# Sums of w_val's low parts in the transposes' banks, a first load in two parts, P.V apart from the scores in two early groups, and new urgencies for the list order

## The chip, the cores and the metric

One core of a Trainium2 chip runs the whole program. The metric is the time of one execution on the device in microseconds (us), the median of several runs. TensorE (PE in the rows) multiplies, VectorE (DVE) and ScalarE (ACT) work elementwise, GpSimd (POOL) helps them out of SBUF, and SyncE (SP) issues the loads and stores.

## The reference, cut to what matters

```python
scores = 1.0 / np.sqrt(D) * np.matmul(q, k.transpose(0, 1, 3, 2))      # B, H, S, D = 4, 8, 768, 64
keep = (pos[None, :] < 8) | ((rel >= 0) & (rel < 96))                  # 8 global keys and 96 local ones
scores = np.where(keep, scores + bias, -1e9)                           # bias: -slope of the head * distance
a = softmax(scores)
x = np.matmul(a, v).transpose(0, 2, 1, 3).reshape(B, S, H * D)
gate = sigmoid(sum(conv_w[k] * xp[:, k:k + S] for k in range(5)))      # causal taps along the sequence
out = (gate * (x @ w_val)) @ w_out                                     # w_val, w_out: 512 x 512
```

## The kernel before, in words

The work falls into 32 groups: four batches, two halves of the sequence of 384 rows (`hf`), four pairs of heads. Four groups with the same batch and half make a phase (`ph`, 8 of them). A group has three steps of 128 query rows, 96 steps in all.

For a group, `load` brings keys and queries (tile `kq`), and `scores` (the row of products that is called S below) fills two PSUM banks `s`. For each step and each head of the pair, VectorE adds the bias and takes the row minimum (`add_bias`, tiles `t` and `mins`), ScalarE takes the exponential and its sum (`expo`, tiles `p` and `sm`), GpSimd or VectorE adds 1e-9 to the sum (`guard`), VectorE inverts it (`recip`, `rs`), and GpSimd or VectorE scales the probabilities (`norm`, written to `p`). TensorE transposes them into one of two banks `pt` (`transpose`), ScalarE or VectorE copies that out (`evac_pt`, tile `a`), and `pv` multiplies with the values, two groups at a time, into the banks `x` (called P.V below). From `x` come the high part `xh` (ScalarE), the low part `xl` (VectorE) and five taps of the convolution (`conv`, tile `gate`; ScalarE does the first, VectorE the rest). Per phase follow `val` (`x @ w_val`, 48 matmuls), the product with the gate (`gated`, tile `g`), its parts `gh` and `gl`, and `outp` (36 matmuls, tile `o`), in two banks that have the tag "moe".

Matrix products of full precision are made from three products of rounded parts, so each weight needs a high and a low part. The weights come as 64-bit floats. `f64_abs`, `f64_op` and `w_high` rebuild them in eight pieces (numbers 0 to 3 are w_val, 4 to 7 w_out), and `w_sum` forms the low part on TensorE as a sum of three products (tile `wsum`), which ScalarE or VectorE copies out. For w_val these sums sit in the "moe" banks, for w_out in the banks of the transposes.

What runs when is set by `Plan`: each operation has an urgency, the engines that may do it with a cost for each, and the operations it depends on. `Plan.order` walks through time: it takes the engine that can start something soonest and gives it the ready operation of least urgency. `SPARE` shifts the choice between engines that may do the same operation. The order that comes out is fixed when the program is built; on the chip each engine works down its own list, and waits where an input is late. From group 4 on, P.V of the pair before is tied to the scores of an odd group: it stands directly ahead of them on TensorE, and it also waits for what they wait for (`ALONE`, `follow`).

`zeros` and `transpose` also issue products of ones whose result is not used (8 at the start, 3 after the first scores, some ahead of early transposes).

Of the kernel before, what the change touches and what calls it, by code (L numbers as in the profile page):

```python
# [15 lines left out]
AX = mybir.AxisListType  # L16
WARM = 8
S_B, PT_B, X_B = 2, 2, 2
U_D1, RAW_B = -5.67, 4
FILL_UNTIL = 80.0  # L20
FILL_N, FILL_TO, U_F = 1, 1, -0.93
W_AT = (-0.83, 5.35, 7.09, 10.66, 17.84, 19.21, 23.25, 35.21)
W_PARTS = (2, 2, 2, 2, 2, 2, 1, 1)
# [3 lines left out]
U_XE, U_XH, U_CV, CV_STEP = -0.29, 0.48, 4.06, 0.71  # L27
U_AM, U_EX, U_RC, U_PT, U_EV, U_MOE = -0.83, 0.3, -4.29, -1.16, 4.27, 19.31
LAG, ALONE = 2, 4
U_L, U_LV, U_WL, U_S, U_HI, U_NM = -21.15, -0.46, -9.19, -2.28, 1.27, -0.88  # L30
U_PH = (-5.11, -0.44, -0.85, -0.71, -0.86, -0.58, -4.31, 2.92)
U_SG, U_GM, GM_STEP, U_GH, U_GL, U_O, VAL_T, O_T, U_OE = 14.07, -1.19, -0.47, 0.06, 0.36, 2.94, 5.39, 4.03, 1.99
PSUM = bass.MemoryType.PSUM
# [26 lines left out]
class Plan:  # L60
# [28 lines left out]
    def order(self, start):  # L89
# [16 lines left out]
        while avail:  # L106
            cands = []
            for i in avail:
# [4 lines left out]
            _, i, e = min(  # L113
                ((ops[i][0], i, e) for t, i, e in cands if e == first[2] and t <= first[0] + 1e-9)
            )
# [23 lines left out]
def attention_moe(ctx, tc, qT, kg, kq0, kq1, va0, va1, v, counts_in, wv, cw, wo, out):  # L139
# [84 lines left out]
    def load(g):  # L224

        b, hf, p = groups[g]
        n = kwidth(hf) + HT
        t = tile_of(("kq", g), [P, KQ], F32, "kq", RAW_B)
        nc.sync.dma_start(t[:, :n], (kq0, kq1)[hf][b, p])
        T["rk", g], T["rq", g] = t[:, : n - HT], t[:, n - HT : n]  # L230

    def load_v(g):
# [8 lines left out]
    for g, (b, hf, p) in enumerate(groups):  # L241
        key = ("L", g)
        plan.add(key, 3 * g + U_L, {SP: 0.5}, lambda e, g=g: load(g), plan.ring("kq", RAW_B, key, [("S", g)]),
                 P * (kwidth(hf) + HT) * 4)
# [127 lines left out]
    def w_sum(i):  # L372

        tag, bufs = ("moe", 2) if i < NC else ("pt", PT_B)
        high = wvh[:, i] if i < NC else woh[:, i - NC]
        ps = tile_of(("wsum", i), [P, DM], F32, tag, bufs, psum)
        nc.tensor.matmul(ps, ident, T[("w", i), "h"].bitcast(F32), start=True, stop=False)
        nc.tensor.matmul(ps, units[:, 1], high, start=False, stop=False)
        nc.tensor.matmul(ps, units[:, 0], T[("w", i), "r"], start=False, stop=True)

    def add_sum(i):
        key, low = ("WS", i), wvl[:, i] if i < NC else wol[:, i - NC]
        bank = plan.ring("moe", 2, key, [("WP", i)]) if i < NC else plan.ring("pt", PT_B, key, [("WP", i)])
        plan.add(key, W_AT[i] + 0.6, {PE: 1.6}, lambda e: w_sum(i), [("WH", i), ("W4", i), ("UNITS",)] + bank)
# [3 lines left out]
    for i in range(2 * NC):  # L388
# [14 lines left out]
        plan.add(("WH", i), u + 0.5, {ACT: 0.52, DVE: 0.335}, lambda e, i=i: w_high(e, i), [("W2", i), ("W3", i)])  # L403
        if i < NC:
            add_sum(i)

# [124 lines left out]
    def s_deps(g):  # L531
        deps = [("L", g)]
        return deps + ([("AM", 3 * (g - 1) + k, j) for k in range(HB) for j in range(2)] if g else [])
# [18 lines left out]
    for g in range(NGRP + LAG):  # L552
        gs = batches.get(g)
        if gs and ALONE <= g < NGRP:
            add_pv(gs, g, pv_cost(gs) + SWITCH, s_deps(g))
        elif gs:
            add_pv(gs, g, pv_cost(gs) + 2 * SWITCH)
        if g < NGRP:
            joined = gs and g >= ALONE
            plan.add(("S", g), 3 * g + U_S, {PE: s_cost(g) + 2 * SWITCH}, lambda e, g=g: scores(g),  # L560
                     s_deps(g) + ([("PV", gs[0])] if joined else []))
            if joined:
                plan.follow(("S", g), ("PV", gs[0]))

    for g, (b, hf, p) in enumerate(groups):
        for k in range(HB):
# [20 lines left out]
            for j in range(2):  # L587
# [5 lines left out]
                     [("NM", s, 0), ("NM", s, 1), ("IOTA",)] + bank, bank=bank)  # L593
            for i in range(NC, 2 * NC):
                if s == WS_AT[i - NC]:
                    add_sum(i)
# [352 lines left out]
def layouts(inputs):  # L949
# [28 lines left out]
    for hf, (lo, hi) in enumerate(((0, P + PER * (HB - 1)), (P + PER * (HB - 1) - TAIL, P + PER * (NB - 1)))):  # L978
        kq.append(np.concatenate([kT[..., lo:hi], qT[..., hf * HT : (hf + 1) * HT]], axis=-1))
        own = slice(0, HB - 1) if hf == 0 else slice(HB - 1, NB - 1)  # L980
        parts = [vs[:, :, :, own].reshape(B, NP, P, -1), vo[:, :, :, own].reshape(B, NP, P, -1)]
# [28 lines left out]
```

## Time and profile before

| what | value |
|---|---|
| median of 3 runs | 278.65 us (278.49 to 278.68) |
| the profiled execution, its own time | 278.04 us |
| its span, first to last instruction | 276.3 us |
| mean granted TensorE clock | 0.994 of full speed |
| TensorE busy with matmuls | 261.1 us (95%) |
| TensorE busy with weight loads | 215.9 us (78%) |
| ScalarE busy | 208.7 us (76%) |
| VectorE busy | 193.7 us (70%) |
| GpSimd busy | 129.9 us (47%) |

The profiled execution took 1.74 us more than its span, which lies ahead of the first and behind the last instruction. Busy times are shares of the whole span: an engine that is full in one stretch and half idle in the next shows a middling share, so the rows further down are taken by stretch. An idle time in a row is that of the engine just before the instruction, and the arrow names what ended it.

### The profile page before, as it was taken

The numbers are of one execution on the slowest core, as the hardware profiler recorded it, in microseconds if no ns is written. First come the engines' busy times: TensorE is split into PE (matmuls) and PEld (weight loads), VectorE is DVE, ScalarE is ACT, GpSimd is POOL, SyncE is SP. The second block draws the span as 40 slices with busy tenths as digits, with TensorE's granted clock in tenths as the row PEclk, the third lists the DMA queues.
The fourth block names the chain that finished last, engine by engine and source line by source line (L and its number), as shares of the span: only waits on it lengthen the run. The fifth ranks groups of instructions, "written<-read, shape, count | busy, mean of one in ns | idle before, by whom it ended". The sixth has DMA issues, their size and how long they took to land.

```text
span 276.3 us, 8766 instructions
## 1 busy us (share of the span) xinstructions
PE 261.1 (95%) x3113; PEld 215.9 (78%) x3114; DVE 193.7 (70%) x762; ACT 208.7 (76%) x700; POOL 129.9 (47%) x323
## 2 busy tenths in 40 slices
PE   7689899898899999999999999999999999999995
PEld 3366587766589788988899788888898888977984
DVE  3878999697938866595949684787849584844610
ACT  4999997897969688787878797887877786854321
POOL 5877526666344633374345633373346544350230
PEclk9899999999999999999999999999999999999999
DMA  6779884251735144421645164523551011001003
GB/s 171 275 240 303 290 302 149 92 151 59 241 121 183 62 149 143 148 94 55 223 116 191 40 193 138 157 66 119 178 187 65 4 76 40 2 2 77 38 2 122
DMA packets 16048, 36.36 MB, mean 132 GB/s; under 512 B 1920, under 2 KB 3968, under 8 KB 16000
## 3 DMA queue, kind: packets, MB, share of 16 engines
q1 hardware_dynamic: 16000, 35.75, 39.2%
q8 instruction: 27, 0.44, 0.7%
q14 instruction: 21, 0.17, 0.2%
HBM read 29.45 MB, written 6.29 MB: 129 GB/s over the span
## 4 chain that ended last, share of the span: by engine, by line
PE 57%; DVE 15%; ACT 2%; issue 1%; POOL 1%; POOLq 0%
PE o L693 23%; PE val L670 12%; PE x L512 7%; DVE gate L622 6%; PE pt L495 6%; PE s L451 5%; PE x L518 4%; DVE t L459 3%; DVE g L677 3%; DVE xl L614 2%; DVE p L484 1%; ACT gate L624 1%; POOL p L484 1%; ACT p L469 1%; ACT ob L704 0%
## 5 line engine op out<-in xcount | busy, mean ns | idle before, releaser
L484 POOL TENSOR_SCALAR p<-p,rs 128x168 f32<-128x168 f32 (+1 forms) x179 | 75.7, 435 | 43.2 <-DVE rs L479 35.4
L469 ACT ACTIVATE p<-t,mins 128x168 f32<-128x168 f32 (+1 forms) x192 | 82.0, 429 | 11.1 <-DVE mins L459 9.9
L622 DVE SCALAR_TENSOR_TENSOR gate<-x,cwt,gate 128x384 f32<-128x384 f32 x128 | 78.5, 614 | 1.0
L459 DVE CUSTOM_DVE_ANT_0 t<-s,bias 128x168 f32<-128x168 f32 (+1 forms) x192 | 56.7, 317 | 9.6 <-PE s L451 9.6
L495 PE MATMUL pt<-ident,p 128*128 128x128 f32 x272 | 49.1, 282 | 4.2 <-POOL p L484 3.3
L476 POOL TENSOR_SCALAR sm<-sm 128x2 f32<-128x2 f32 x92 | 19.5, 212 | 63.2 <-ACT p L469 57.3
L670 PE MATMUL val<-xh,wvh 128*128 128x384 f32 x128 | 47.6, 372 | 1.2 <-DVE g L677 1.2
L161 ACT COPY a<-pt 128x384 f32<-128x384 f32 (+1 forms) x96 | 43.6, 454 | 4.8 <-PE pt L495 4.8
L495 PEld LDWEIGHTS pt<-ident,p 128*128 128x128 f32 x272 | 34.1, 142 | 16.5 <-POOL p L484 9.2
L693 PE MATMUL o<-woh,gh 128*128 128x512 f32 (+1 forms) x100 | 42.5, 425 | 1.1 <-DVE g L677 0.9
L670 PE MATMUL val<-xh,wvl 128*128 128x384 f32 x128 | 43.1, 337 | 0.0
L670 PE MATMUL val<-xl,wvh 128*128 128x384 f32 x128 | 43.1, 337 | 0.0
L684 POOL TENSOR_TENSOR gl<-g,gh 128x384 fp32r<-128x384 f32 x29 | 29.2, 1010 | 26.8 <-ACT gh L161 25.7
L693 PE MATMUL o<-wol,gh 128*128 128x512 f32 (+1 forms) x100 | 38.9, 389 | 1.2 <-ACT wol L161 1.2
L693 PE MATMUL o<-woh,gl 128*128 128x512 f32 (+1 forms) x100 | 38.6, 386 | 0.0
L469 ACT ACTIVATION_READ_ACCUMULATOR p<-t,mins 128x1 f32 x192 | 37.1, 193 | 0.0
L451 PE MATMUL s<-kq 64*64 64x104 f32 (+3 forms) x1088 | 34.2, 262 | 3.0 <-DMA kq<-in_kq 3.0
L451 PEld LDWEIGHTS s<-kq 64*64 64x64 f32 x1088 | 30.3, 133 | 7.6 <-issue 4.0
L614 DVE TENSOR_TENSOR xl<-x,xh 128x384 fp32r<-128x384 f32 x32 | 17.3, 555 | 25.8 <-ACT gate L624 16.1
L161 ACT CAST xh<-x 128x384 fp32r<-128x384 f32 x32 | 15.1, 484 | 20.8 <-PE x L518 20.8
L479 DVE RECIPROCAL rs<-sm 128x2 f32<-128x2 f32 x96 | 15.5, 161 | 21.7 <-POOL sm L476 21.0
L670 PEld LDWEIGHTS val<-xh,wvh 128*128 128x128 f32 x128 | 24.1, 188 | 3.9 <-DVE g L677 2.4
(155 smaller groups left out, 373.1 us busy)
## 6 DMA issues: line engine op xcount, KB each, us to landing
kq<-in_kq SPq DMA_DIRECT2D x16, 444.0 KB, 4.3
kq<-in_kq SPq DMA_DIRECT2D x16, 392.0 KB, 4.3
va<-in_va SPq DMA_DIRECT2D x16, 384.0 KB, 4.2
out<-ob SPq DMA_DIRECT2D x24, 256.0 KB, 2.2
va<-in_va SPq DMA_DIRECT2D x16, 320.0 KB, 4.3
w<-in_wv SPq DMA_DIRECT2D x8, 256.0 KB, 4.4
w<-in_wo SPq DMA_DIRECT2D x4, 256.0 KB, 3.8
w<-in_wo SPq DMA_DIRECT2D x2, 512.0 KB, 3.9
```

Source lines behind the costliest of these rows:

```text
L161: nc.scalar.copy(dst, src)
L451: nc.tensor.matmul(s[rows, u : u + w], T["rq", g][r, k * P + half * QH : k * P + (half + 1) * QH], T["rk", g][r, c : c + w], start=True, s ...
L459: nc.vector.tensor_tensor_reduce(out=t[:, :n], in0=T["s", s // HB, s % HB, j][:, :n], in1=bias[:, h, :P] if n == P else bias[:, h, P:], op ...
L469: nc.scalar.activation(T["p", s][:, j, :n], T["t", s, j][:, :n], AF.Exp, bias=mins[:, s, j : j + 1], scale=-1.0, accum_out=T["sm", s][:, j ...
L476: engine(e).tensor_scalar(out=sm, in0=sm, scalar1=1e-9, scalar2=1.0, op0=ALU.add, op1=ALU.mult)
L484: engine(e).tensor_scalar(out=pr, in0=pr, scalar1=rs, scalar2=1.0, op0=ALU.mult, op1=ALU.mult)
L495: nc.tensor.transpose(pt[:, i * P : (i + 1) * P], pr[:, c : c + P], ident)
L614: engine(e).tensor_sub(tile_of(("xl", g), [P, HT], F32R, "xl", XH_B), T["x", g][:, HIST:], T["xh", g])
L622: nc.vector.scalar_tensor_tensor(out=gt, in0=src, scalar=w, in1=gt, op0=ALU.mult, op1=ALU.add)
L670: nc.tensor.matmul(T["val", ph, m], (wvh, wvh, wvl)[r][:, m, c * P : (c + 1) * P], (T["xh", g], T["xl", g], T["xh", g])[r], start=(c == 0 ...
L684: engine(e).tensor_sub(tile_of(("gl", ph, m), [P, HT], F32R, "gl", 5), T["g", ph, m], T["gh", ph, m])
L693: nc.tensor.matmul(T[key][:, cols], (T["gh", ph, c], T["gl", ph, c], T["gh", ph, c])[r][:, rows], (woh, woh, wol)[r][:, c, cols], start=(c ...
```

## The change

Six things change; what is computed stays the same.

1. The sums of w_val's low parts use the banks of the transposes, as those of w_out did. They are placed by step (`WS_AT`).
2. The first load of keys and queries is issued in two parts: columns 0 to 127 of both, then the rest. For that the array of the first half is padded to two equal parts of 400 columns. The scores of step 0 need the first part alone.
3. P.V is tied to the scores of an odd group only from group 9 on (`JOIN`), where it was from group 5 on. In groups 5 and 7 it is now an operation of its own.
4. At the start there are 10 products of ones and not 8, and after the first scores 12 and not 3.
5. All urgencies have new values, and `SHIFT` adds to each kind of operation a value of its own for each of the 8 phases.
6. `SPARE` has new values.

```diff
-WARM = 8
+WARM = 10
-FILL_N, FILL_TO, U_F = 1, 1, -0.93
+FILL_N, FILL_TO, U_F = 4, 1, -1.44
-WS_AT = (15, 19, 22, 24)
-SPARE = {'vector': 0.8, 'gpsimd': 0.02, 'scalar': -0.96}
+WS_AT = (1, 4, 7, 10, 15, 19, 22, 24)
+SPARE = {'vector': 0.91, 'gpsimd': 0.02, 'scalar': -1.19}
-LAG, ALONE = 2, 4
+LAG = 2
+JOIN = (0, 0, 0, 0, 1, 1, 1, 1, 1, 1, 1, 1, 1, 1, 1, 1)
+SHIFT = {
+    'AM': (-3.57, 0.0, 0.0, 0.0, 0.45, 0.94, 0.07, 3.21),
...
+        if key[0] in SHIFT:
+            urgency += SHIFT[key[0]][key[1] // PER_PHASE[key[0]]]
...
-        nc.sync.dma_start(t[:, :n], (kq0, kq1)[hf][b, p])
+        if g == 0:
+            load_part(slice(0, P))
+        else:
+            nc.sync.dma_start(t[:, :n], (kq0, kq1)[hf][b, p, :, :n])
...
+        if g == 0:
+            plan.add(("LB", 0), U_L, {SP: 0.5}, lambda e: load_part(slice(P, kwidth(0))))
...
-        tag, bufs = ("moe", 2) if i < NC else ("pt", PT_B)
+        ps = tile_of(("wsum", i), [P, DM], F32, "pt", PT_B, psum)
...
-        if gs and ALONE <= g < NGRP:
-            add_pv(gs, g, pv_cost(gs) + SWITCH, s_deps(g))
-        elif gs:
-            add_pv(gs, g, pv_cost(gs) + 2 * SWITCH)
+        join = JOIN[g // 2] if gs and g < NGRP else 0
+        pv_in = [d for h in gs for d in pv_deps(h)] if join == 2 else []
+        if join != 2 and gs:
+            add_pv(gs, g, pv_cost(gs) + SWITCH * (2 - join), s_deps(g) if join else [])
```

The order that comes out of it differs most in the first 10 groups. On ScalarE the exponentials of group 5 (the `p` tiles with the numbers 798 before and 730 now) stand as follows. Before, from the copy of step 12's transposes on:

```order
L161 COPY a_679<-pt_666 128x384
L332 ACTIVATE ('w', 4)_y<-w_495 128x512
L663 ACTIVATE gate_542<-gate_542 128x384 x2
L161 COPY a_730<-pt_690 128x384
L161 CAST woh<-('w', 4)_h 128x512
L161 CAST xh_763<-x_653 128x384
L161 COPY hist<-x_653 128x4
L161 CAST xh_768<-x_697 128x384
L161 COPY hist<-x_697 128x4
L624 ACTIVATE gate_542<-x_653,cwt 128x384
L332 ACTIVATE ('w', 5)_y<-w_613 128x512
L469 ACTIVATE p_798,sm_799<-t_0_787,mins 128x168
```

Now, from the copy of step 10's transposes on:

```order
L188 COPY a_678<-pt_636 128x384
L370 ACTIVATE ('w', 4)_y<-w_516 128x512
L188 CAST wvl<-wsum_664 128x512
L699 ACTIVATE gate_582<-gate_582 128x384
L188 COPY a_728<-pt_713 128x384
L504 ACTIVATE p_730,sm_731<-t_0_720,mins 128x168
L188 COPY a_741<-pt_723 128x384
L504 ACTIVATE p_730,sm_731<-t_1_733,mins 128x168
```

The pieces of weights 4 and 5, the high parts `xh` of groups 2 and 3 and their convolution moved from ahead of group 5's exponentials to behind them. Ahead of the first of them ScalarE now has one `f64_abs`, two `xh`, two small copies to `hist`, one `w_high`, three copies of transposes, one first tap and one tanh less, and one bias more. At the first exponential of group 9 the two lists hold the same work but for that one bias.

On TensorE the second place is around the scores of group 7 (`s` with the numbers 1040 before and 974 now) and P.V of groups 4 and 5 (`x` 894 and 965 before, 962 and 1052 now). Before:

```order
L495 MATMUL pt_984<-ident,p_913 128x128 x3
L512 MATMUL x_894<-a_679,va_486 64x128 x2
L512 MATMUL x_965<-a_890,va_544 64x128 x2
...
L518 MATMUL x_965<-a_967,va_544 64x64 x2
L451 MATMUL s_0_1040<-kq_662 64x168
...
L495 MATMUL pt_1074<-ident,p_939 128x128 x3
```

Now:

```order
L486 MATMUL s_0_974<-kq_705 64x168
...
L530 MATMUL pt_1000<-ident,p_870 128x128 x3
L729 MATMUL o_0_1012<-woh,gh_0_904 128x512
...
L416 MATMUL wsum_1042<-('w', 5)_r,units 128x512
L547 MATMUL x_962<-a_741,va_444 64x128 x2
L547 MATMUL x_1052<-a_935,va_561 64x128 x2
```

The scores of group 7 stood behind the transposes of step 18 and that P.V, and now stand ahead of both. P.V of groups 2 and 3 moved in the same way from ahead of the scores of group 5 to behind them.

The third place is TensorE's list near the end, at the last P.V (`x` 4509 before, 4551 now), the product `val` of phase 7 and `rmt`, the transpose of the check of the row minima. Before:

```order
L518 MATMUL x_4509<-a_4571,va_3862 64x64 x4
L693 MATMUL o_2_4574<-woh,gh_2_4483 128x512
...
L773 MATMUL rmt<-ident,row_max 1x128
L693 MATMUL o_2_4574<-woh,gh_3_4517 128x512
...
L670 MATMUL val_0_4629<-xh_4370,wvh 128x384
```

Now:

```order
L809 MATMUL rmt<-ident,row_max 1x128
L706 MATMUL val_0_4607<-xh_4430,wvh 128x384
...
L553 MATMUL x_4551<-a_4602,va_3875 64x64 x4
L706 MATMUL val_0_4607<-xh_4436,wvh 128x384
...
L706 MATMUL val_0_4607<-xh_4646,wvh 128x384
```

Six matmuls of `outp` that stood behind the last P.V now stand ahead of it, so `val` follows it at once; between the last P.V and the first `val` that needs its result (`xh` 4646) there are 12 other matmuls of `val`. On VectorE the list holds 6 normalisations of probabilities where it held 13, and no `guard` where it held 4; the rest went to GpSimd.

## Rows read from the trace of the kernel before

**Rows 1.** Windows: start:end, length, busy us (count) by engine, clock, DMA

```profile
5.79:39.09 33.30, 28.73 (x393) 20.83 (x387) 28.98 (x124) 31.81 (x112) 22.17 (x54) 0.95 0.85 285
...
39.09:70.43 31.34, 28.68 (x372) 21.60 (x372) 26.14 (x96) 26.52 (x89) 18.20 (x39) 1.00 0.40 130
...
96.58:156.89 60.31, 59.57 (x767) 51.62 (x768) 44.01 (x180) 48.21 (x166) 28.29 (x73) 1.00 0.41 133
```

**Rows 2.** The same view of two short stretches

```profile
50.00:54.70 4.70, 3.97 (x112) 3.38 (x113) 2.22 (x8) 3.40 (x11) 2.96 (x8) 1.00 0.30 112
...
65.00:70.43 5.43, 4.90 (x110) 3.83 (x111) 3.01 (x11) 4.05 (x13) 3.19 (x7) 1.00 0.18 51
```

**Rows 3.** Timeline: start us, us, engine line op, count [idle before <-releaser]

```profile
0.78 3.57 PE L254 MATMUL warm<-const-bfloat16-1.0 128*128 128x512 bf16 x8 [0.78 <-PEq L1000]
...
5.56 1.02 PE L451 MATMUL s<-kq 64*64 64x128 f32 x32 [1.20 <-DMA kq<-in_kq]
...
6.48 0.23 DVE L308 TENSOR_SCALAR dist<-m,counts 128x8 f32<-128x8 f32 x1
...
6.51 0.82 PE L254 MATMUL warm<-const-bfloat16-1.0 128*128 128x512 bf16 x3
...
9.12 1.14 PE L451 MATMUL s<-kq 64*64 64x128 f32 x32 [1.78 <-DMA kq<-in_kq]
...
12.06 0.27 DVE L459 CUSTOM_DVE_ANT_0 t<-s,bias 128x128 f32<-128x128 f32 x1
```

**Rows 4.** Windows by 5 us: the slice with a low clock

```profile
10.00:15.00 5.00, 4.53 (x26) 2.63 (x18) 4.47 (x25) 4.44 (x17) 4.14 (x10) 0.66 0.69 226
```

**Rows 5.** ScalarE's timeline: one of each kind, and the exponential opening group 5

```profile
5.79 1.77 ACT L320 ACTIVATE bias<-dist 128x128 f32<-128x128 f32 x7 [3.24 <-DVE dist L302]
...
33.20 0.52 ACT L161 COPY a<-pt 128x384 f32<-128x384 f32 x1
...
33.55 0.73 ACT L332 ACTIVATE ('w', 4)_y<-w 128x512 f32<-128x512 f32 x1
...
34.14 0.97 ACT L663 ACTIVATE gate<-gate 128x384 f32<-128x384 f32 x2
...
35.66 0.62 ACT L161 CAST woh<-('w', 4)_h 128x512 fp32r<-128x512 f32 x1 [0.19 <-DVE ('w', 4)_h L343]
...
36.52 0.48 ACT L161 CAST xh<-x 128x384 fp32r<-128x384 f32 x1 [0.24 <-PE x L518]
...
37.69 0.58 ACT L624 ACTIVATE gate<-x,cwt 128x384 f32<-128x384 f32 x1 [0.18 <-DVE xl L614]
...
39.09 0.44 ACT L469 ACTIVATE p<-t,mins 128x168 f32<-128x168 f32 x1
```

**Rows 6.** Timeline of ScalarE: two of its waits

```profile
46.13 0.44 ACT L469 ACTIVATE p<-t,mins 128x168 f32<-128x168 f32 x1 [0.81 <-DVE mins L459]
...
53.91 0.48 ACT L161 CAST xh<-x 128x384 fp32r<-128x384 f32 x1 [0.89 <-PE x L518]
```

**Rows 7.** Chain of waits (start us, us, what), then PE's timeline

```profile
89.47 1.00 DVE p L484
...
92.42 0.50 PE L693 MATMUL o<-woh,gh 128*128 128x512 f32 x1 [0.23 <-DVE g L677]
```

**Rows 8.** Waits of PE up to 100 us: total, times, longest us

```profile
PE pt L495 <- ACT wol L161: 0.3, 1, 0.3
```

**Rows 9.** Timeline: one sum of a low part, and its copy

```profile
18.14 1.02 PE L377 MATMUL wsum<-('w', 1)_h,ident 128*128 128x512 f32 x2
...
19.67 0.59 ACT L161 CAST wvl<-wsum 128x512 fp32r<-128x512 f32 x1 [0.28 <-PE wsum L379]
```

**Rows 10.** Timeline and chain of waits near the end

```profile
253.26 0.92 PE L518 MATMUL x<-a,va 64*64 64x64 f32 x24
...
255.27 0.56 DVE L614 TENSOR_TENSOR xl<-x,xh 128x384 fp32r<-128x384 f32 x1 [3.34 <-ACT gate L624]
...
255.86 8.55 PE val L670 x48
```

More of the change, by code (lines that the diff above doesn't have):

```diff
@@ L113, in order @@
             _, i, e = min(
-                ((ops[i][0], i, e) for t, i, e in cands if e == first[2] and t <= first[0] + 1e-9)
+                ((ops[i][0], i, e) for t, i, e in cands if e == first[2] and t <= first[0] + LOOK[e])
             )
@@ L228, in load, with load_part @@
         t = tile_of(("kq", g), [P, KQ], F32, "kq", RAW_B)
-        nc.sync.dma_start(t[:, :n], (kq0, kq1)[hf][b, p])
+        if g == 0:
+            load_part(slice(0, P))
+        else:
+            nc.sync.dma_start(t[:, :n], (kq0, kq1)[hf][b, p, :, :n])
         T["rk", g], T["rq", g] = t[:, : n - HT], t[:, n - HT : n]
+    def load_part(cols):
+        n = kwidth(0)
+        dst, src = (x[:, : 2 * n].rearrange("p (two n) -> p two n", two=2) for x in (T["kq", 0], kq0[0, 0]))
+        nc.sync.dma_start(dst[:, :, cols], src[:, :, cols])
     def load_v(g):
@@ L531, in s_deps @@
     def s_deps(g):
-        deps = [("L", g)]
+        deps = [("L", g)] + ([] if g else [("LB", 0)])
         return deps + ([("AM", 3 * (g - 1) + k, j) for k in range(HB) for j in range(2)] if g else [])
@@ L553, in attention_moe @@
         gs = batches.get(g)
-        if gs and ALONE <= g < NGRP:
-            add_pv(gs, g, pv_cost(gs) + SWITCH, s_deps(g))
-        elif gs:
-            add_pv(gs, g, pv_cost(gs) + 2 * SWITCH)
+        join = JOIN[g // 2] if gs and g < NGRP else 0
+        pv_in = [d for h in gs for d in pv_deps(h)] if join == 2 else []
+        if join != 2 and gs:
+            add_pv(gs, g, pv_cost(gs) + SWITCH * (2 - join), s_deps(g) if join else [])
         if g < NGRP:
-            joined = gs and g >= ALONE
             plan.add(("S", g), 3 * g + U_S, {PE: s_cost(g) + 2 * SWITCH}, lambda e, g=g: scores(g),
-                     s_deps(g) + ([("PV", gs[0])] if joined else []))
-            if joined:
-                plan.follow(("S", g), ("PV", gs[0]))
+                     s_deps(g) + ([("PV", gs[0])] if join == 1 else pv_in))
+        if join == 2:
+            add_pv(gs, g, pv_cost(gs) + SWITCH, [("S", g)])
+        if join:
+            plan.follow(*((("S", g), ("PV", gs[0])) if join == 1 else (("PV", gs[0]), ("S", g))))
     for g, (b, hf, p) in enumerate(groups):
@@ L593, in attention_moe @@
                      [("NM", s, 0), ("NM", s, 1), ("IOTA",)] + bank, bank=bank)
-            for i in range(NC, 2 * NC):
-                if s == WS_AT[i - NC]:
+            for i in range(2 * NC):
+                if s == WS_AT[i]:
                     add_sum(i)
@@ L979, in layouts @@
         kq.append(np.concatenate([kT[..., lo:hi], qT[..., hf * HT : (hf + 1) * HT]], axis=-1))
+        if hf == 0:
+            kq[0] = np.pad(kq[0], [(0, 0)] * 3 + [(0, hi - lo - HT)])
         own = slice(0, HB - 1) if hf == 0 else slice(HB - 1, NB - 1)
```

30 lines of the change are left out of this document (17 added, 13 removed), and 15 rows, old and new, of the table SHIFT.

## The prediction, made before the changed kernel ran

> **What bounds the kernel now.** I read the busy times by stretch first, cutting the span at the two points where the order before and after the change holds the same work. From 96.58 us on TensorE is the limit: in a period of two phases it is busy 59.57 of 60.31 us, with ScalarE at 48.21 and VectorE at 44.01 [rows 1]. Whatever the new urgencies do there can give at most the 0.74 us that TensorE idles per period. Its weight loads are busy 51.62 us of that period [rows 1], but the matmuls of `val` run 8.55/48 = 0.178 us apart with no gap [rows 10], and an order changes the gaps alone. The Trainium skill, Perfetto Trace Analysis, Identifying the Most-Contended Engine, holds that TensorE's matmul busy time is a poor measure of headroom and its weight loads' busy share a better one; by it the room would be 60.31 - 51.62 = 8.7 us a period. I weigh that as a rival below. Up to the first exponential of group 5, at 39.09 us [rows 5], it is another engine: ScalarE is busy 31.81 of 33.30 us, TensorE 28.73 [rows 1]. Between there and the first exponential of group 9, at 70.43 us, nothing is full: TensorE 28.68, ScalarE 26.52, VectorE 26.14 of 31.34 us [rows 1]. So a reader should look for a gain in the first 70 us, and ask of each edit whether it shortens ScalarE's list or its waits.
>
> Next I read those waits. ScalarE idles 33.30 - 31.81 = 1.49 us in the first stretch and 31.34 - 26.52 = 4.82 us in the second. Two holes hold 2.68 us of the latter: 50.00 to 54.70 (4.70 - 3.40 = 1.30) and 65.00 to 70.43 (5.43 - 4.05 = 1.38); VectorE idles 2.48 and 2.42 us in the same holes [rows 2]. Both are a joined P.V: TensorE waits for the last transposes before it, the scores stand behind it, and so VectorE has no scores and ScalarE no `x`, for which it waits 0.89 us at 53.91 [rows 6].
>
> **The change, part by part.** All sums are made against the profiled execution, 278.04 us, which is 0.61 us below the median of 278.65 us.
>
> First load in two parts: nothing. The scores of group 0 start at 5.56 us, when their load has landed [rows 3]; a smaller load may bring that forward. But the first `add_bias` stands behind the distances on VectorE, the last of which runs from 6.48 to 6.71 us [rows 3], and the new list keeps that order. If the distances were done sooner, the first scores would be worth up to their own wait, 1.20 us [rows 3]; the ends are 0 and -1.20, and I take 0, since the cover is in the list. The extra issue puts the next loads back a little; group 1's scores, which wait for theirs, have the slack of the next paragraph.
>
> Products of ones: nothing. Two more at the start take 2 x 3.57/8 = 0.89 us and end at 5.24, ahead of 5.56. Twelve after the first scores take 12 x 0.82/3 = 3.28 us at the pace of the three there now, so group 1's scores start at about 9.8 us, where they wait for a load until 9.12 [rows 3]. Their reader, the next `add_bias`, starts at 12.06 [rows 3], and the scores would end at 10.9: the slack of 1.1 us hides it. At the pace of the first eight (0.446 each) the twelve end at 11.9 and the scores at 13.0, a loss of 0.9 us; so 0 to +0.9, and I take 0, since the three ran right after scores, as the twelve will.
>
> The clock: from 10 to 15 us the granted clock is 0.66 [rows 4], between the levels of 1.2 and 2.4 GHz; TensorE had idled 1.78 us ahead of the scores of group 1 [rows 3]. At those levels that is (1 - 0.66)/0.5 x 5 = 3.4 us at half pace, 1.7 us of TensorE's work. The twelve products fill that idle time, so the fall may go. ScalarE idles only 5.00 - 4.44 = 0.56 us in that slice [rows 4], so this is worth 0 to -0.56; I take 0, because ScalarE's list sets the pace there.
>
> ScalarE's list: one bias more, 1.77/7 = 0.25 us [rows 5]. It takes 0.25 us off any gain.
>
> The order up to group 9. Ahead of group 5's exponentials ScalarE loses, by [rows 5], 0.73 + 2 x 0.48 + 0.62 + 3 x 0.52 + 0.58 + 0.97/2 less 0.25, which is 4.7 us (the two copies to `hist` are left out). In a stretch in which ScalarE is 96% busy that is time: group 5 starts at about 34.4 us and not 39.09. Nothing is saved by it alone, since the same 4.7 us come back before group 9. What it can save is idle time there: ScalarE and VectorE now hold work that is ready while TensorE does P.V. The joined P.V of groups 4 and 5 no longer stands ahead of group 7's scores, so the hole at 50 to 54.7 us should close: -1.30. With group 5 some 4.7 us ahead, the wait of an exponential for `mins` at 46.13 [rows 6] should go: -0.81. The hole at 65 us stays, because P.V of groups 6 and 7 still stands ahead of group 9's scores behind the first transposes of group 8. The other 1.3 us I leave. The bounds are 0 (every wait comes back elsewhere) and -4.82 (none does).
>
> Sums in the transposes' banks: +0.30. A sum holds one of two banks from 18.14 to 20.26 us, 2.1 us [rows 9], and transposes behind it must alternate. The four sums of w_out have always stood there, and they cost TensorE's transposes 0.3 us of waiting in all [rows 8]; I take the same for the four of w_val. The bounds are 0 and 4 x 2.1 = 8.5 us.
>
> Later phases. Of the seven normalisations and four `guard`s that leave VectorE, two with their `guard` stand directly ahead of a product with the gate that TensorE waits for, behind the last `add_bias` of groups 12 and 28: the one at 89.47 us takes 1.00 us, and TensorE idles 0.23 us at 92.42 for it [rows 7]. VectorE's list sheds 1.2 us there, GpSimd gains 0.4: -2 x 0.23 = -0.46, at most the 0.74 us per period [rows 1].
>
> The end. The last P.V now runs directly into `val`. Before, its low part `xl` is done at 255.83 us (255.27 and 0.56), and that P.V ends at 254.18 (253.26 and 0.92) at the latest [rows 10]: 1.7 us. The 12 matmuls of `val` in between take 12 x 8.55/48 = 2.1 us [rows 10]. So 0, with 0.4 us to spare; without that cover it costs up to 1.7 us. Behind it both lists end alike.
>
> Sum: 0.25 - 1.30 - 0.81 + 0.30 - 0.46 = -2.02 us, so 276.02 us for a profiled execution and 278.65 - 2.02 = 276.6 us for the median.
>
> **The rivals.** Later phases have more room than 0.74 us a period: the 8.7 us outside weight loads hold time that another order can win. If a tenth of it came back in each of the three periods behind 96.58 us, that would be 2.6 us more than my sum, 274.0 us. For it speaks only that the two shares differ; against it, that TensorE idles 0.74 us and that `val` runs without a gap, so most of the 8.7 us lie inside matmuls, where no order reaches.
>
> The lead is spent fully: no wait of ScalarE comes back up to group 9. Then the gain is 4.82 - 0.25 - 0.30 + 0.46 = 4.7 us, 273.9 us. For it speaks that all three engines have slack in that stretch; against it, that the joined P.V of groups 6 and 7 keeps its place.
>
> The lead is given back: P.V of groups 2 to 5 come later, so `xh`, `xl` and the taps come later too, ScalarE and VectorE idle for them instead, and at group 9 the lists are level. Then +0.25 + 0.30 - 0.46 = +0.1 us: 278.7 us, no change. For it speaks that both lists hold the same work at group 9; against it, that the work now waits ready rather than late.
>
> The banks decide: transposes of steps 12 and 13 stand behind the sum of weight 3 and ahead of P.V of groups 2 and 3, and TensorE takes its list in order, so a copy of that sum that is late on a full ScalarE stops everything behind. At half a hold per sum, 4 x 1.06 = 4.2 us against a gain of 2.32 without the 0.30: 280.6 us, slower. It turns the sign from (2.32 + 0.56)/4 = 0.72 us of waiting per sum on. Against it speaks the 0.3 us that four such sums cost now.
>
> **How the numbers follow.** A measurement of this kernel tells about 0.2%, 0.56 us, from no change. My forecast, a gain of 0.7 to 3.2 us (275.4 to 277.9 us), has a chance of 0.55; the lead spent fully 0.08; more room later 0.02; no change, 0.17; the banks, 0.18. So faster 0.65, same 0.17, slower 0.18. The range leaves out the outer part of the large gain and nearly all of the slow case: 274.6 to 279.2 us holds 0.55 + 0.06 (a lead nearly spent) + 0.17 + 0.02 = 0.80. The open prices are in it: 0.9 us for the twelve products, 0.56 us for the clock.
>
> **What would show it.** First exponential of group 5 at 34 to 35 us; first of group 9 at 68.3 to 69 us, with ScalarE's idle time from 39 us on down by some 2 us; group 7's scores ahead of P.V with VectorE busy in it; first `add_bias` still at 6.8 us; the clock at 1.00 up to 15 us; no idle time of TensorE ahead of the first matmul of `outp` at the place of 92.42; `val` of phase 7 without a gap. I am wrong if the transposes of steps 11 to 14 wait for a copy of a sum, if group 1's scores end after 12 us, or if group 9 opens at 70 us or later in spite of group 5's lead.

## The result, and the profile after

The changed kernel takes 274.08 us (median of four executions, 273.92 to 274.36), the kernel before 278.62 beside it: a ratio of 0.9839 [0.9822, 0.9856], 4.5 us less. The forecast was 276.6 us with a range of 274.6 to 279.2: the direction was right, the size was more than twice the forecast, and the time lies below the range. The profiled execution took 274.04 us, of them 272.2 in the span. Its page, busy time and share by engine:

```profile
span 272.2 us, 8800 instructions
...
PE 260.0 (96%) x3125; PEld 216.7 (80%) x3127; DVE 188.4 (69%) x752; ACT 209.4 (77%) x701; POOL 133.1 (49%) x332
```

The timeline of its first 13 us (start us, us, engine line op, count, idle before and who ended it) answers to [rows 3]:

```profile
0.78 4.13 PE L292 MATMUL warm<-const-bfloat16-1.0 128*128 128x512 bf16 x10 [0.78 <-PEq L1038]
...
4.84 1.38 PE L486 MATMUL s<-kq 64*64 64x128 f32 x32
...
6.02 0.23 DVE L346 TENSOR_SCALAR dist<-m,counts 128x8 f32<-128x8 f32 x1
...
6.15 2.80 PE L292 MATMUL warm<-const-bfloat16-1.0 128*128 128x512 bf16 x11
...
6.40 0.29 DVE L494 CUSTOM_DVE_ANT_0 t<-s,bias 128x128 f32<-128x128 f32 x1 [0.16 <-PE s L486]
...
10.53 1.16 PE L486 MATMUL s<-kq 64*64 64x128 f32 x32 [1.58 <-DMA kq<-in_kq]
...
11.79 0.29 DVE L494 CUSTOM_DVE_ANT_0 t<-s,bias 128x128 f32<-128x128 f32 x1 [0.29 <-PE s L486]
```

The distances end 0.46 us sooner, at 6.25, and the first `add_bias` starts 0.39 sooner, at 6.40. Group 1's scores start 1.4 us later, behind a load that is issued and lands later, and their reader waits 0.29 us for them; it starts at 11.79 all the same, where [rows 3] have 12.06.

Windows of the same execution (start:end, length, then busy us and count of TensorE, its weight loads, VectorE, ScalarE, GpSimd; granted clock, DMA share, GB/s). The first four answer to [rows 1] and [rows 4]. They are cut at the first exponentials of groups 5 and 9, and behind 93 us at P.V of groups 10 and 18, where the changed list has the transposes of one step less between the cuts (3 matmuls). The last three are used below:

```profile
5.32:35.11 29.79, 25.52 (x330) 17.62 (x332) 24.36 (x113) 27.85 (x102) 20.92 (x53) 1.00 0.85 280
35.11:67.80 32.69, 31.42 (x439) 25.30 (x439) 29.77 (x105) 30.11 (x98) 19.50 (x40) 1.00 0.48 163
93.68:153.05 59.37, 58.86 (x764) 51.32 (x765) 42.15 (x175) 48.06 (x165) 29.28 (x76) 1.00 0.42 135
10.00:15.00 5.00, 4.47 (x74) 3.20 (x74) 3.90 (x22) 3.87 (x16) 3.42 (x9) 1.00 0.87 293
...
65.68:104.13 38.45, 37.61 (x444) 31.30 (x435) 27.51 (x115) 31.81 (x109) 18.84 (x51) 1.00 0.45 148
140.06:154.95 14.89, 14.89 (x200) 13.33 (x196) 11.41 (x48) 12.20 (x43) 9.84 (x24) 1.00 0.36 113
...
205.61:272.20 66.59, 62.54 (x619) 54.33 (x618) 34.95 (x120) 37.23 (x112) 22.78 (x49) 0.99 0.10 38
```

Group 5 opens at 35.11 us (39.09 before), group 9 at 67.80 (70.43 before). In this execution the clock doesn't fall between 10 and 15 us.

To find where time goes, the trace must be cut where TensorE has the same work behind it. By the two lists it has that at the scores of groups 9, 14, 19, 21 and 28. The windows of the kernel before between those cuts:

```profile
68.31:107.36 39.05, 38.12 (x443) 31.36 (x435) 28.89 (x116) 31.60 (x109) 17.95 (x48) 1.00 0.45 149
143.23:158.79 15.56, 15.32 (x201) 13.39 (x196) 12.65 (x50) 12.10 (x43) 9.25 (x22) 1.00 0.35 107
...
209.45:276.30 66.85, 62.99 (x619) 54.33 (x618) 35.60 (x122) 36.60 (x112) 22.55 (x47) 1.00 0.10 38
```

So 68.31 - 65.68 = 2.63 us come ahead of group 9's scores, 39.05 - 38.45 = 0.60 between groups 9 and 14, 15.56 - 14.89 = 0.67 between 19 and 21, 66.85 - 66.59 = 0.26 behind group 28, and nothing in the other stretches (groups 21 to 28 take 50.66 us in both). The forecast had 1.56 us ahead of group 9 and 0.46 behind it; the trace has 2.6 and 1.5.

### The profile page after: what moved, and what is told of

Its sections match the earlier page's. It is cut to its first block, busy times and chain, and to the rows that moved or that the text cites. A ratio compares the mean times of both kernels' runs of the same rounds, so it can differ in the third digit from the quotient of the medians.

```text
span 272.2 us, 8800 instructions
## 1 busy us (share of the span) xinstructions
PE 260.0 (96%) x3125; PEld 216.7 (80%) x3127; DVE 188.4 (69%) x752; ACT 209.4 (77%) x701; POOL 133.1 (49%) x332
## 4 chain that ended last, share of the span: by engine, by line
PE 76%; DVE 8%; DMA 6%; ACT 4%; issue 2%; SPq 2%; POOL 1%; POOLq 0%; ACTq 0%
PE o L729 25%; PE val L706 19%; PE pt L530 9%; PE s L486 9%; PE x L547 8%; DMA kq<-in_kq 6%; PE x L553 5%; DVE gate L658 4%; ACT p L504 2%; DVE xl L650 1%; DVE t L494 1%; PE wsum L414 1%; DVE g L713 1%; ACT gate L660 1%; POOL p L519 1%
## 5 line engine op out<-in xcount | busy, mean ns | idle before, releaser
L519 POOL TENSOR_SCALAR p<-p,rs 128x168 f32<-128x168 f32 (+1 forms) x186 | 79.9, 441 | 39.7 <-DVE rs L514 28.6
L530 PE MATMUL pt<-ident,p 128*128 128x128 f32 x272 | 47.2, 278 | 1.4 <-ACT wvl L188 0.5
L720 POOL TENSOR_TENSOR gl<-g,gh 128x384 fp32r<-128x384 f32 x28 | 28.5, 1020 | 32.2 <-ACT gh L188 31.0
```

Source lines behind the costliest of these rows:

```text
L519: engine(e).tensor_scalar(out=pr, in0=pr, scalar1=rs, scalar2=1.0, op0=ALU.mult, op1=ALU.mult)
L530: nc.tensor.transpose(pt[:, i * P : (i + 1) * P], pr[:, c : c + P], ident)
L720: engine(e).tensor_sub(tile_of(("gl", ph, m), [P, HT], F32R, "gl", 5), T["g", ph, m], T["gh", ph, m])
```

## The experiments

In e7, e8 and e12 the list of the order is made anew by `Plan`; in all others it is written out, so that an edit acts alone and moves nothing else. A run is compared by its median, the ratio stands against the kernel before on the same chip.

**Which half holds it: e3 and e4.** Both splice the two lists at the scores of group 9; in short:

```
order = first[: first.index(("S", 9))]
order += [op for op in second if op not in order]
```

> The changed kernel's order up to the scores of group 9, with all edits of its start, and from there on the order of the kernel before. Theory (2.6 to 2.9 us are won ahead of group 9's first exponential and carried on, the rest, 1.6 us, by the later order): 275.5 to 276.1. Rival (later waits take the lead back when the order behind it isn't made for it): 276.5 to 278.5. Second rival (the later phases gain only from what lies ahead of them): 274.1 to 274.5.

> The kernel before up to the scores of group 9, load, products of ones and banks as before, and from there on the order of the changed kernel. Theory (the later order alone is worth 1.3 to 1.9 us: 0.9 between the points 96.58 and 156.89 us, 0.7 behind 217.13): 276.7 to 277.3. Rival (the later order only fits a lead made earlier): 278.2 to 279.0, no gain. My prediction's term for this order was 0.46 us: 278.2.

e3 took 275.51 us, 0.9897 [0.9877, 0.9917]; e4 277.26, 0.9953 [0.9939, 0.9968]. The halves are worth 3.0 and 1.3 us, and they add up: the later order needs no early lead.

**The first load: e1.**

```diff
-        if g == 0:
-            load_part(slice(0, P))
-        else:
-            nc.sync.dma_start(t[:, :n], (kq0, kq1)[hf][b, p, :, :n])
+        nc.sync.dma_start(t[:, :n], (kq0, kq1)[hf][b, p, :, :n])
```

> The changed kernel with its own order written out, but the load of group 0 in one part as before. Theory (the two parts bring the first scores, 5.56 to 4.84 us, and the first exponential, 8.02 to 7.00 us, forward, and that 1.0 us is carried to the end): the first exponential goes back to about 8.0 us and the time rises by 0.7 to 1.0 us over the changed kernel's 274.08, to 274.8 to 275.1. Rival (the start is covered by later waits, as my prediction had it, and the order alone made the lead): the time stays within 0.3 us of 274.1. Second rival (the first exponential came early because the counts landed at 3.55 and not 4.02 us, whatever the load): it stays at about 7.0 us here too.

273.97 us, 0.9831 [0.9814, 0.9848]: the two parts are worth nothing. The first exponential came at 7.26 us, not at 8.02 as before, with the load in one part; ahead of it there had stood a piece of weight 0 of 0.66 us, which the new order puts behind it. My theory for this run was that the two parts make the earlier start and that it is carried to the end. The first half falls: 0.76 of the 1.02 us are there without them. Whether an earlier start is carried to the end was not tested.

**P.V joined later: e8.** One number of the kernel before.

```diff
-LAG, ALONE = 2, 4
+LAG, ALONE = 2, 8
```

> The kernel before with one number changed: P.V is joined to the scores from group 9 on and not from group 5 on. The list differs up to the scores of group 9 and is that of before behind them. Theory (this edit closes the hole at 50 to 54.7 us, 1.30, and the wait at 46.13, 0.81, and the hole at 65 us, 1.38, needs another one): 1.3 to 2.1 us less, 276.4 to 277.3. Rival (all of the early gain of 2.6 us comes from this edit): 275.8 to 276.0. Second rival (the lead is given back ahead of group 9): 278.3 to 278.8.

276.20 us, 0.992 [0.9892, 0.9948], 2.4 us less by the medians. ScalarE's timeline of e8 has the first exponentials of groups 5 and 9 at

```profile
34.76 0.46 ACT L469 ACTIVATE p<-t,mins 128x168 f32<-128x168 f32 x1
...
68.39 0.40 ACT L469 ACTIVATE p<-t,mins 128x128 f32<-128x128 f32 x1
```

where the prediction had 34 to 35 and 68.3 to 69. This one number makes most of the early lead, 70.43 - 68.39 = 2.04 us of 2.63, as long as the hole at 50 us and the wait at 46.13 together (1.30 + 0.81). The windows of e8, from ScalarE's first bias to group 5 and from there to group 9, show where that time lies:

```profile
5.60:34.76 29.16, 24.92 (x315) 17.06 (x305) 25.21 (x117) 28.33 (x103) 21.23 (x53) 0.94 0.83 279
34.76:68.39 33.63, 32.26 (x439) 25.04 (x438) 29.84 (x103) 29.82 (x98) 19.55 (x41) 1.00 0.45 156
```

ScalarE idles 3.81 us in the second window, 1.01 less than before, and 0.83 in the first, 0.66 less than before. Another 0.19 us is an earlier start (5.60 and not 5.79), and 0.18 less busy time. Both named waits are gone, but P.V comes later now, and new waits stand in their place, the longest for `xl`:

```profile
57.71 0.58 ACT L624 ACTIVATE gate<-x,cwt 128x384 f32<-128x384 f32 x1 [0.88 <-DVE xl L614]
```

**The banks: e7 and e12.** e7 takes the changed kernel and puts the four sums back; e12 takes the kernel before and moves them.

```diff
-        ps = tile_of(("wsum", i), [P, DM], F32, "pt", PT_B, psum)
+        tag, bufs = ("moe", 2) if i < NC else ("pt", PT_B)
+        ps = tile_of(("wsum", i), [P, DM], F32, tag, bufs, psum)
...
```

> The changed kernel with the four sums of w_val in the banks of val again, and the list made anew with the changed urgencies; up to the scores of group 9 the list differs, from there on every engine's list is the changed kernel's. Theory (in the transposes' banks the sums cost no waiting, and leave the banks of val free, so that val starts ahead of the fourth sum and TensorE has work for its waits): the time rises by 0.5 to 2 us, to 274.6 to 276.1. Rival (my prediction's price: the sums hold the transposes up by 0.30 us): the time falls to 273.8. Second rival (the place makes no difference): 273.9 to 274.3.

> The kernel before with one edit: the four sums of w_val take the banks of the transposes, behind steps 1, 4, 7 and 10, and the list is made anew with the old urgencies; it differs up to the scores of group 9 and is that of before behind them. My prediction's price: 0.30 us more, 278.8 to 279.0. Rival (the sums and their copies stop transposes and P.V, 0.72 us and more each): 281 us or more, with group 9's scores 2.9 us later or worse. Second rival (free banks for val alone make TensorE's early list better): 276 to 278.

e7: 278.06 us, 0.9987 [0.997, 1.0005]; e12: 280.94, 1.0082 [1.0066, 1.0098]. Either half of the pair of banks and urgencies without the other loses: 4.0 us from the changed kernel, 2.3 us from the kernel before. Each of these prices is that of the banks together with the list that `Plan` makes for them, which differs up to the scores of group 9. In e12 the place is the one that the prediction named, the transposes ahead of P.V of groups 2 and 3. TensorE's timeline there, with the sum of weight 3 between transposes:

```profile
30.85 1.13 PE L376 MATMUL wsum<-('w', 3)_h,ident 128*128 128x512 f32 x2 [0.40 <-ACT a L161]
...
33.62 0.52 PE L492 MATMUL pt<-ident,p 128*128 128x128 f32 x3 [0.85 <-POOL p L481]
34.41 0.52 PE L492 MATMUL pt<-ident,p 128*128 128x128 f32 x3 [0.28 <-ACT a L161]
35.11 0.81 PE L487 MATMUL pt<-const-bfloat16-1.0 128*128 128x512 bf16 x2 [0.18 <-ACT a L161]
```

Group 9's scores start at 70.56 us in e12, 2.25 later than before. What TensorE waits for here are copies of other transposes (`a`: 0.40, 0.28 and 0.18 us) and a normalisation on GpSimd (0.85). No wait of e12's TensorE ahead of group 9 is put down to the copy of a sum of w_val. In the changed list the sum of weight 3 stands directly ahead of the scores of group 5, and there the transposes of step 12 do wait for its copy, once:

```profile
33.84 0.52 PE L530 MATMUL pt<-ident,p 128*128 128x128 f32 x3 [0.49 <-ACT wvl L188]
```

**The wait of `outp`: e5 and e9.** Both give instructions of VectorE to GpSimd in the list of the kernel before: e5 a guard and the normalisation of j = 1 at steps 37, 61 and 85, e9 the normalisation of j = 0 at steps 34, 58 and 82.

```diff
-    (("NM", 34, 0), "vector"),
+    (("NM", 34, 0), "gpsimd"),
```

> The kernel before with its own order, in which only three guards and three normalisations (steps 37, 61 and 85, each pair ahead of the last product with the gate of a phase) go from VectorE to GpSimd, at the same places of the list. Theory (each of the three stalls costs what the weight load of outp waits, 0.5 to 0.6 us, and the refilling of the array, 0.67 in all between two points with the same work): 3 x 0.5 to 3 x 0.67, so 276.5 to 277.0 us. Rival (the price is TensorE's idle row of 0.23 us, as my prediction had it): 278.5 - 0.7 = 277.8. Second rival (GpSimd is late with six more instructions and the transposes wait instead): 278.5 or more.

> The kernel before with its own order, in which only three normalisations (j = 0 of steps 34, 58 and 82) go from VectorE to GpSimd. In the trace of before each takes 1.00 to 1.03 us on VectorE, two convolution taps and an add_bias ahead of the product with the gate that frees the bank of outp. Theory (VectorE's list is what makes outp wait there; its weight load then waits 0.5 to 0.6 us and the array refills, so each place costs 0.67 us, the last one 0.26 because the end has slack of its own): 0.67 + 0.67 + 0.26 = 1.6 us less, 276.8 to 277.3. Rival (TensorE's idle row of 0.23 us is the whole price): 3 x 0.23 = 0.7 less, 277.8 to 278.0. Second rival (TensorE's own changed order there is what removes the wait, not VectorE's list): 278.4 to 278.8.

e5: 278.97 us, 1.0009 [0.9994, 1.0024], no gain: those pairs stand behind the `gated` that TensorE waits for. They are the pairs with their `guard` that the prediction described, so its description was aimed at the wrong instructions. e9: 277.16 us, 0.9938 [0.9919, 0.9957], 1.5 us less. The wait in the kernel before, by its timeline at the second of the three places (TensorE, its weight load, VectorE, GpSimd):

```profile
149.60 1.00 POOL L684 TENSOR_TENSOR gl<-g,gh 128x384 fp32r<-128x384 f32 x1 [0.43 <-ACT gh L161]
149.67 1.03 DVE L484 TENSOR_SCALAR p<-p,rs 128x168 f32<-128x168 f32 x1
...
152.05 0.55 DVE L677 SCALAR_TENSOR_TENSOR g<-gate,val 128x384 f32<-128x384 f32 x1
152.08 0.34 PE L670 MATMUL val<-xh,wvl 128*128 128x384 f32 x1
...
152.65 0.19 PEld L693 LDWEIGHTS o<-woh,gh 128*128 128x128 f32 x1 [0.56 <-DVE g L677]
152.66 0.50 PE L693 MATMUL o<-woh,gh 128*128 128x512 f32 x1 [0.24 <-DVE g L677]
...
153.88 0.48 PE L693 MATMUL o<-woh,gh 128*128 128x512 f32 x1
```

And the same place in e9:

```profile
151.50 0.55 DVE L677 SCALAR_TENSOR_TENSOR g<-gate,val 128x384 f32<-128x384 f32 x1
...
152.50 0.34 PE L670 MATMUL val<-xh,wvl 128*128 128x384 f32 x1
152.51 0.19 PEld L693 LDWEIGHTS o<-woh,gh 128*128 128x128 f32 x1
...
152.69 0.39 PE L693 MATMUL o<-woh,gh 128*128 128x512 f32 x1
...
153.62 0.48 PE L693 MATMUL o<-woh,gh 128*128 128x512 f32 x1
```

From the last matmul of `val` to the `outp` behind the next transposes it is 153.88 - 152.08 = 1.80 us in the one and 153.62 - 152.50 = 1.12 in the other. The idle row says 0.24. The rest lies in starts: `outp` starts 0.58 us behind `val` and not 0.19, the second matmul of `outp` 0.33 behind the first and not 0.22, and the transposes take 0.42 us and not 0.25: they wait for a normalisation whose `recip` stands behind the late product with the gate on VectorE. The windows of e9 over the three places say the same, against 9.58, 9.59 and 39.05 us between the same cuts in the kernel before:

```profile
149.63:158.54 8.91, 8.91 (x126) 7.98 (x129) 6.25 (x28) 6.66 (x23) 6.76 (x15) 1.00 0.16 49
209.19:218.09 8.90, 8.90 (x126) 7.98 (x129) 6.25 (x28) 6.64 (x23) 6.76 (x15) 1.00 0.01 4
69.43:107.79 38.36, 37.66 (x445) 31.43 (x436) 27.84 (x115) 31.76 (x109) 18.45 (x49) 1.00 0.46 151
```

0.67 to 0.69 us at each of three places, 2.05 in all. The median shows 1.5 of it; the profiled execution of e9 opened group 9's scores at 69.43 us, after a late start (last section), where the others with that list had 68.05 to 68.76. How many of its other executions started late isn't known.

**The products of ones: e2, e10, e11 and e15.** e2, e10 and e11 take the changed kernel and go back to eight and three, to ten and three, and to eight and twelve. e15 gives the kernel before ten and twelve.

```diff
-WARM = 8
+WARM = 10
-FILL_N, FILL_TO, U_F = 1, 1, -0.93
+FILL_N, FILL_TO, U_F = 4, 1, -0.93
```

> The changed kernel with its own order written out, but 8 products of ones at the start and 3 after the first scores, as before. Theory (the clock stays at 1.00 through 10 to 15 us because of the products, but ScalarE sets the pace there): the granted clock from 10 to 15 us falls to about 0.66 again and the time rises by 0 to 0.3 us, to 274.1 to 274.4. Rival (the clock is a part of the gain): it rises by 0.5 us or more, to 274.6 or above, and the first exponential of group 9 is later than 67.80 by that much. Second rival (the products cost TensorE time ahead of group 1's scores): the time falls by 0.3 us or more.

> The changed kernel with its own order, ten products of ones at the start and three, not twelve, after the first scores. Theory (the twelve bridge the wait for the load of group 1, and without them the granted clock falls between 11 and 14 us, which costs what the run with eight and three lost): 275.1 to 275.6. Rival (the first ten are what matters, by the pace of the first scores): 274.0 to 274.3. Second rival (each half is worth a part): 274.5 to 274.9.

> The changed kernel with its own order, eight products of ones at the start, not ten, and twelve after the first scores. Theory (the twelve alone keep the clock): 274.0 to 274.3. Rival (the first ten are what matters): 275.1 to 275.6. Second rival (each half is worth a part): 274.5 to 274.9.

> The kernel before with its own order and ten and twelve products of ones in place of eight and three. Theory (the ones are worth the same there as in the changed kernel): 0.4 to 1.3 us less, 277.3 to 278.2. Rival (my prediction: ScalarE's list hides the clock): 278.4 to 278.8. Second rival (the twelve put group 1's scores back, which here start at about 8.5 to 9.1 us and not at 10.5): 279.0 to 280.0.

e2: 275.39 us, 0.9887 [0.987, 0.9904]; e10: 274.71, 0.9859 [0.9834, 0.9885]; e11: 274.53, 0.9847 [0.9829, 0.9865]. e15: 277.97, 0.9981 [0.9972, 0.999], and its twelve executions lie between 277.82 and 278.10, where the kernel before went from 277.79 to 279.55 beside it. Together they are worth 0.5 us in the kernel before and 1.3 in the changed one. Neither half alone can be told from the changed kernel, since the intervals of e10 and e11 take in its ratio. In e10 the load of group 1 came late, the clock fell, and it stayed at the lower level of 1.2 GHz for the scores, by the window and the timeline:

```profile
10.00:16.00 6.00, 4.81 (x40) 3.71 (x41) 3.76 (x23) 3.73 (x16) 3.15 (x9) 0.50 0.86 295
```

```profile
10.97 1.95 PE L486 MATMUL s<-kq 64*64 64x128 f32 x32 [3.42 <-DVE cw_r L460]
```

Those 32 matmuls take 1.16 us in the changed kernel. Its twelve products shorten TensorE's idle time there to 1.58 us, and the clock stays.

The granted clock isn't the whole of it. The profiled executions of e4, e5, e9 and e12 have the eight and three products of the kernel before, and read 1.00 from 10 to 15 us all the same; that of e8 reads 0.66. Over the 75 executions of the kernel before that were taken beside these runs, the 34 with a mean granted clock of 0.994 or less have a median of 278.54 us, the 41 others 278.64. In e10 the time does follow the clock, from 274.03 us at 0.999 to 276.26 at 0.985; in e2 it doesn't (275.18 at 0.994, 275.81 at 0.998).

**Do three edits make the whole gain: e13.** The kernel before with `ALONE = 8` and the list of e8, the three normalisations of e9 and the ones of e15; its load, banks and urgencies stay.

> The kernel before with three edits alone: P.V joined to the scores from group 9 on (the list made anew with the old urgencies), the three normalisations of steps 34, 58 and 82 on GpSimd, and ten and twelve products of ones in place of eight and three. First load, banks and urgencies are those of before. Theory (these three are the whole gain, and they add): 278.6 - 2.4 - 1.5 - 0.4 to 1.3, so 273.4 to 274.3 us, as good as the changed kernel's 274.1. Rival (the banks with their urgencies, and the first load, hold a part of it): 274.8 to 276.0. Second rival (the ones gain nothing here): 274.5 to 274.8.

274.13 us (274.04 to 274.38), 0.9844 [0.9826, 0.9862]: level with the changed kernel. By their ratios, times 278.6 us, the three parts alone are 2.23, 1.73 and 0.53 us, together 4.49; e13 has 4.35 and the changed kernel 4.49. The two come there by different ways. These are the first and the last of e13's windows between the cuts with the same work:

```profile
66.29:104.67 38.38, 37.70 (x444) 31.44 (x435) 27.84 (x115) 31.74 (x109) 18.42 (x49) 1.00 0.45 151
...
206.10:272.20 66.10, 62.52 (x619) 54.43 (x618) 34.55 (x121) 36.75 (x112) 23.03 (x48) 1.00 0.10 38
```

At the scores of group 9 e13 is 0.61 us behind the changed kernel (66.29 and 65.68). From there to the end of the span it is 0.61 us shorter (205.91 and 206.52), 0.49 of it behind group 28.

**The end: e6, e14 and e16.** e6 and e14 follow the changed list up to the scores of group 29 and 28 and the list of before from there, e14 with the normalisation of step 82 on GpSimd. e16 is e14 with the load of e1.

> The changed kernel up to the scores of group 29, and the order of the kernel before from there to the end. Theory (behind group 29 the changed order needs 0.4 us more than the old one for the same work: 57.00 against 57.26 us with one product of outp, 0.67 us, less to do): 273.6 to 273.8. Rival (the difference comes from the point of the cut, not from the order of the tail): 274.0 to 274.2. Second rival (the old tail brings its own wait of outp for the gate back): 274.4 to 274.8.

> The changed kernel up to the scores of group 28, and from there to the end the order of the kernel before with the normalisation of step 82 (j = 0) on GpSimd. Theory (between those scores and the end the changed kernel needs 9.59 + 57.00 = 66.59 us, this order 8.90 + 57.3 = 66.2 by the run with the three normalisations moved): 0.4 less than the changed kernel, 273.6 to 273.8. Rival (the ends are level): 274.0 to 274.2.

> The changed kernel with the first load in one part (273.97 us when tried alone) and the end of e14_end (0.43 us less between the scores of group 28 and the end by its trace, 274.04 in its median). Theory (the two add): 273.4 to 273.7, faster than both kernels. Rival (either is level with the changed kernel within what can be measured): 273.9 to 274.2.

e6: 274.06 us, 0.9833 [0.9809, 0.9857]. e14: 274.04, 0.9833 [0.9811, 0.9855], though its trace is 0.43 us shorter behind group 28 (66.16 and 66.59). The changed list does one set of `outp` more ahead of group 29's scores, three matmuls 0.23 us apart, and so takes 9.59 us from group 28 to 29 as the kernel before did, though the wait of `outp` there is gone; behind group 29 it gets only 0.26 us back (57.00 and 57.26). e16: 273.80 (273.63 to 273.92), 0.9824 [0.981, 0.9838]: the shortest time of all, 0.3 us under the changed kernel, which is less than can be told from no change.

## Why the prediction was right or wrong

**First load: right.** Nothing was forecast, and e1 shows nothing. Its cover was not quite the one named, since the distances came 0.46 us sooner too.

**Products of ones and the clock: the size was wrong.** I took 0 for both because ScalarE's list sets the pace and idles only 0.56 us in that slice, with -0.56 as the far end for the clock. e15 gives 0.5 us in the kernel before, which is inside that end; e2 gives 1.3 in the changed one, which is not. The step that failed is the bound of 0.56 us from ScalarE's idle time in one slice of one trace: in e10 the load of group 1 came later, and the clock stayed low for 6 us and not for the 3.4 that I had counted. By which wait the loss reaches the end was not followed, and since the time of the kernel before doesn't follow its granted clock, the clock may be the smaller part of it. The slack argument for the twelve products held: group 1's reader started at 11.79 and not later than before.

**One bias more and the order up to group 9: the way was right, the size in part luck.** The join was to close the hole at 50 us and the wait at 46.13, 2.11 us; e8 shows 2.04 in its trace, groups 5 and 9 open in e8 where they were forecast, and both waits are gone. But only 1.01 of the 2.04 us is ScalarE's idle time behind group 5, where I put all of it: the rest came back, in the main as waits for `xl` (0.55 and 0.88) and `g` (0.52), and 1.03 us were won elsewhere, of them 0.66 in idle time ahead of group 5.

**The hole at 65 us: wrong.** I left it because P.V of groups 6 and 7 keeps its place. It does, but from the scores of group 8 to those of group 9 TensorE idles nothing in the changed kernel, 0.35 us in e8 and 0.96 before: behind the sum of weight 6 four sets of `outp` stand ahead of the last transposes there, where two stood. That is the likely home of the early gain beyond e8's; no run took it alone. On ScalarE the hole is only smaller: its wait for `x` there is 0.81 us, where it was 1.28.

**Sums in the banks: the size was wrong in both directions.** Moved alone they cost 2.3 us (e12), 0.56 us per sum, at the steps that the rival "the banks decide" named. Its mechanism, a late copy of a sum, isn't what that trace shows; which of the waits there reaches the end stays open. With the urgencies that belong to them they cost nothing in the end (e13 does without both and is level). The price of 0.30 was that of four sums of w_out at places where the list had room; it is the list that sets it.

**Later phases: this is the term that failed most.** -0.46 was forecast; e9 has -1.5 in the median and 2.05 in the trace, the changed kernel 1.5. Four steps went wrong. I counted two places and there are three, behind the first `add_bias` of groups 12, 20 and 28. I described the instructions as pairs with their `guard` behind the last `add_bias` of groups 12 and 28, and those gain nothing (e5); the row that I priced, at 89.47 us, is another normalisation, that of step 34, and it is the one that counts (e9). I priced each at TensorE's idle row of 0.23 us, and it costs 0.67. And I took the 0.74 us of idle time per period for the most that an order could give. The 0.67 us lies below that, but 15.32 - 14.89 = 0.43 us of it was booked as busy between groups 19 and 21, for the same matmuls, so idle time is no such bound. Here the wait showed in part as longer matmuls (0.50 us for the first of `outp` and not 0.39), and most of its length stood in the row of the weight load (0.56).

**The end: no change, as forecast,** for no order of it that was tried moves the median by 0.3 us. By the traces the changed order of the end gives away some 0.4 us (e14).

**The rivals.** "More room later" gave 274.0 us and "the lead is spent fully" 273.9, beside the measured 274.1, and neither is what happened. The lead at group 9 is 2.6 us, not 4.3. The later room is three waits and not a share of the weight loads' free time: the matmuls of `val` still run 0.17 us apart. Yet on one point the page behind the first rival was the better guide. The Trainium skill, Perfetto Trace Analysis, Identifying the Most-Contended Engine, warns that TensorE's matmul busy time doesn't tell headroom; the 0.43 us above, waiting that was booked as busy, agree. I held the busy share against it, which is the very thing it warns of.

By what was measured the sum is -2.23 (join) - 1.73 (normalisations) - 0.53 (ones) = -4.49 us. Of it the prediction had 2.11 + 0.46 + 0, and took 0.55 away for a bias and the banks. That this sum meets the changed kernel's 4.49 is in part luck, since by the traces that kernel wins more ahead of group 9 and less behind it than the three edits do. Of the signs that it named, the clock, the idle time at 92.42 and ScalarE's idle time from 39 us on (4.82 to 2.58 us) came true, group 5 opened 0.11 us behind its window, the first `add_bias` came at 6.40 and not at 6.8, `val` of phase 7 has one gap of 0.16 us, and group 9 opened half a microsecond ahead of its window. One sign of being wrong came true as well: the transposes of step 12 wait 0.49 us for the copy of a sum. The lead stands in spite of it.

## What to carry to other kernels

Price a wait of TensorE between two cuts with the same work, by the row of its weight load and by the starts behind it, and not by its idle row. When a change makes many moves at once, run the old kernel with one number changed: here three small edits hold as much as the whole change, and the rest of it adds nothing to the time that can be measured. When a sum meets the measurement, look at its terms in the trace: here the join met its size half by other waits than the ones named. Two changes that need each other, such as a place for the sums and the urgencies around it, can each look like a loss alone.

## What was not expected of the hardware

A normalisation of 128x168 on VectorE took 1.03 us where it started beside a GpSimd subtraction of 1.00 us (the rows at 149.60 and 149.67 above). In the changed kernel the same operation took, by VectorE's timeline,

```profile
153.82 0.31 DVE L519 TENSOR_SCALAR p<-p,rs 128x168 f32<-128x168 f32 x1
...
230.71 0.63 DVE L519 TENSOR_SCALAR p<-p,rs 128x168 f32<-128x168 f32 x1
```

The second of these started late in such a subtraction, by GpSimd's timeline:

```profile
230.22 1.02 POOL L720 TENSOR_TENSOR gl<-g,gh 128x384 fp32r<-128x384 f32 x1
```

In the traces of the two kernels eight single normalisations of VectorE start while such a subtraction runs. Each ends 0.10 or 0.11 us behind the end of the subtraction, however late it started; the others take 0.31 to 0.46 us.

The convolution's taps, whose input `x` lies in PSUM, kept their 0.61 to 0.62 us beside the same subtraction in e9. The Trainium skill, Advanced Engine Details and Errata, VectorE Performance Modes, says that GpSimd instructions and VectorE instructions that use two read ports block each other; these eight normalisations agree, but no run took the subtraction away. It would explain why moving three instructions of some 0.3 us sped up VectorE's list by a microsecond each.

TensorE's pace at the start differs between executions of the same list, and the row of the granted clock doesn't always show it. In e9 it reads 1.00 in every microsecond from 8 to 18, yet group 1's scores took twice the 1.0 to 1.2 us of most other runs (2.49 us in e4):

```profile
8.65 2.32 PE L451 MATMUL s<-kq 64*64 64x128 f32 x32 [0.49 <-DMA kq<-in_kq]
```

What sets this stays open. With the ten and twelve products e15 spreads by only 0.28 us between its shortest and longest time, but e14, which has them too, by 1.22 us, so they don't always remove the spread.
